# Down product of a two-level Strassen-like token pair: blocks taken in another order, closing sums split by row tile

## The chip, the cores and the metric

The kernel runs on one core of one Trainium2 chip. The metric is the device time of one execution in microseconds (us), from the kernel's runs on the chip; the median of three runs of the kernel before is 1055.15 us (1053.54 to 1056.74). The engines are named as the profile names them: PE is the matrix engine, PEld its weight loads, DVE VectorE, ACT ScalarE, POOL GpSimd and SP the engine that issues the DMAs.

## The reference

Attention with a bias, a SwiGLU layer and a SiLU layer follow each other; everything is float32. Only the last is touched here:

```python
def _moe2_ref(x, w_in, w_out):          # x: 2304 x 512, w_in: 512 x 2048, w_out: 2048 x 512
    h = x @ w_in
    g = h * (1.0 / (1.0 + np.exp(-h)))
    return (g @ w_out).astype(np.float32)

def reference(**kw):
    attn_out = _attn_ref(**attn_kwargs)  # 4 x 8 x 576 x 64
    x = attn_out.transpose(0, 2, 1, 3).reshape(B * S, H * D)
    x = _moe_ref(x=x, **moe_kwargs)      # (silu(x @ w_gate) * (x @ w_val)) @ w_out
    return _moe2_ref(x=x, **moe2_kwargs)
```

## The kernel before, in words

Attention and the SwiGLU layer take the first 655 us or so; the change touches only the last layer behind them, `up2` (L607) and `down2` (L651). Every float32 operand is held as two parts, a rounded one (the "cut", by ACT) and the remainder (one subtraction by POOL), and a product is three matmuls: rounded by rounded, rounded by remainder, remainder by rounded. A product of 2 x 2 blocks is computed with seven block products instead of eight, in sums and differences of blocks.

The tokens are done in three thirds (`TG`), each third as two halves of 384 tokens. The hidden columns go in eight steps per third, 24 steps in all. Two steps `a` and `b` and one `down2` make what is here called a **round**; there are twelve, 0 to 11, and rounds 0 to 3, 4 to 7 and 8 to 11 belong to one third each.

`up2` (one step): seven block products of 6 matmuls each, the positions xi 0 to 6, into four PSUM banks; the outputs of some are read while the bank goes on accumulating (xi 0 and 1 are copied by ACT as `s0` and `s1` at L629, and xi 2 then adds into the bank of xi 0). From the banks DVE forms `w` and `u3` (L633, L636) and adds `w` to the others in place (L639, L646), POOL adds `w` to `u3` (L637, `u <- u,w` in the trace), and ACT applies SiLU (L611), which gives `u0` to `u3`. DVE then takes differences of these: `t1 = u1 - u0` (a "token difference"), `t2 = u3 - t1`, `u1 = u3 - u1`, `t4 = u2 - t2` (`h_sub`, L605). Seven operands are cut for the down product by `h_cut` (L596: ACT at L107, then POOL at L600): B11 from `u0`, B22 from `u3`, T1 from `t1`, B21 from `u2`, T2 from `t2`, T3 from the new `u1`, T4 from `t4`. `t1`, `t2`, `t4`, `u3` and `w` have one buffer each, so the next step writes them only when the step before has been read.

`down2` (one round): seven block products, listed in `DOWN` (L42) with the name of the sum, the operand, the weight, the block and the PSUM bank. Each has two row tiles m = 0, 1 of 6 matmuls (3 for step a, 3 for step b), so the fourteen places x2m = 2x + m are 84 matmuls. Two or three products share a bank: the bank goes on accumulating, and DVE adds what it holds after each product to a sum in SBUF (`tt` at L694, `acc <- po,acc`, under the line L654 of the lambda; in rounds 0, 4 and 8 ACT copies it instead, L692). The next matmul into that bank waits for this read. When a third ends (rounds 3, 7, 11), closing sums between those SBUF sums (`close`, L662, `acc <- acc,acc`) give the four output blocks, which SP stores (L660): POOL does them for m = 0 and DVE for m = 1, in the first places of the next round, or inside `down2` in round 11.

The order on each engine is the order in which the code is written: the list `fill` (L949 to L984) hangs further work behind a place, ("u", step, xi) or ("d", round, x2m). In this way the cuts for the down product are spread, and in rounds 3 and 7 the next third's inputs are cut (`x2_cut`, L555: POOL at L560, 128 x 768), four of them at x2m 5, 7, 9 and 11.

## Time and profile before

| | |
|---|---|
| median of three runs | 1055.15 us |
| the profiled execution's own time | 1056.26 us |
| its span, first to last instruction | 1054.5 us |
| PE busy | 1012.4 us, 96% of the span |
| PEld busy | 935.4 us, 89% |
| POOL busy | 638.8 us, 61% |
| DVE busy | 584.7 us, 55% |
| ACT busy | 547.3 us, 52% |
| mean granted TensorE clock | 0.984 |

PE is nearly always busy, so the time can only move where PE waits. A row of the waits tells for how long in all, how often and at most how long an engine sat idle until another one ended. In a timeline each row has a start, a duration, the engine, the line, the operation with output <- input, and in brackets the idle time in front of it with what ended it.

### The profile page before, as it was taken

Reading aid. Unit: us, or ns where it says so; the run is one execution under the profiler, and the core shown is the slowest. Engines: PE = TensorE matmul, PEld = TensorE weight load, DVE = VectorE, ACT = ScalarE, POOL = GpSimd, SP = SyncE. Lnnn points to the kernel's source line nnn. Section 1 sums busy time; section 2 is a strip of 40 time slices with the busy share of each in tenths; the row PEclk is TensorE's granted clock in tenths of the full one; section 3 lists DMA queues with packets and bytes.
Section 4 is the critical chain, followed back from the end, with each engine's and each line's share of the span. In section 5 each row is a group of like instructions: output and inputs, shape, how many; then the busy total and the mean of one; then the engine's idle time right before and its main releaser. Section 6 shows DMA issues by size and latency. Waiting matters only on the chain.

```text
span 1054.5 us, 19518 instructions
## 1 busy us (share of the span) xinstructions
PE 1012.4 (96%) x6864; PEld 935.4 (89%) x6864; DVE 584.7 (55%) x1456; ACT 547.3 (52%) x1272; POOL 638.8 (61%) x797
## 2 busy tenths in 40 slices
PE   8889999999999999999999999999998999979997
PEld 5468998899898899898999999999998999979996
DVE  5877868635746545636533232446674466744555
ACT  6768878525665445656424542552445534455331
POOL 4667756615866656747435663655688556875456
PEclk8989999999999999999999999999998999999999
DMA  8578797758779799668486867976567765677651
GB/s 227 146 247 293 263 332 254 257 188 256 276 284 270 252 321 310 254 217 291 166 306 239 309 257 290 396 285 264 192 217 281 302 247 202 226 261 279 217 202 61
DMA packets 81618, 267.17 MB, mean 253 GB/s; under 512 B 9904, under 2 KB 29360, under 8 KB 66160
## 3 DMA queue, kind: packets, MB, share of 16 engines
q1 hardware_dynamic: 81520, 265.93, 71.7%
q8 instruction: 54, 0.88, 0.3%
q14 instruction: 44, 0.36, 0.1%
HBM read 208.15 MB, written 57.75 MB: 252 GB/s over the span
## 4 chain that ended last, share of the span: by engine, by line
PE 69%; POOL 9%; issue 5%; DMA 3%; ACT 3%; DVE 2%; POOLq 0%; SPq 0%; DVEq 0%; ACTq 0%
PE pgv L485 9%; PE pgv L487 8%; PE pgv L486 8%; POOL h L600 6%; PE po L485 5%; PE po L688 5%; PE po L486 5%; PE po L487 5%; PE po L689 4%; PE po L685 4%; PE pv L319 4%; PE psc L208 3%; PE ptr L278 3%; PE pu L623 2%; PE pu L627 2%
## 5 line engine op out<-in xcount | busy, mean ns | idle before, releaser
L485 PE MATMUL pgv<-xt,wt 128*128 128x288 f32 x768 | 230.2, 300 | 0.4 <-DVE wraw L383 0.4
L487 PE MATMUL pgv<-xt,wt 128*128 128x288 f32 x768 | 226.9, 295 | 0.0
L486 PE MATMUL pgv<-xt,wt 128*128 128x288 f32 x768 | 226.8, 295 | 0.0
L600 POOL TENSOR_TENSOR h<-u,h 128x384 fp32r<-128x384 f32 x96 | 107.4, 1123 | 110.0 <-ACT h L107 105.9
L485 PEld LDWEIGHTS pgv<-xt,wt 128*128 128x128 f32 x768 | 144.7, 188 | 11.3 <-DVE m L225 5.9
L107 ACT ACTIVATE h<-u 128x288 fp32r<-128x288 f32 (+1 forms) x192 | 92.6, 482 | 103.0 <-DVE u L497 96.5
L486 PEld LDWEIGHTS pgv<-xt,wt 128*128 128x128 f32 x768 | 144.8, 189 | 0.0
L487 PEld LDWEIGHTS pgv<-xt,wt 128*128 128x128 f32 x768 | 144.6, 188 | 0.2 <-issue 0.2
L499 POOL TENSOR_TENSOR h<-u,h 128x288 fp32r<-128x288 f32 x96 | 79.4, 830 | 88.2 <-ACT h L107 86.0
L688 PE MATMUL po<-h,wt 128*128 128x384 f32 x336 | 115.7, 344 | 15.6 <-POOL h L600 15.6
L685 PE MATMUL po<-h,wt 128*128 128x384 f32 x336 | 115.1, 343 | 3.7 <-DVE acc L654 2.2
L623 PE MATMUL pu<-x,wt 128*128 128x384 f32 x330 | 113.6, 344 | 3.8 <-ACT s L629 3.0
L485 PE MATMUL po<-h,wt 128*128 128x288 f32 x384 | 114.8, 299 | 0.0
L689 PE MATMUL po<-h,wt 128*128 128x384 f32 x336 | 114.2, 340 | 0.0
L486 PE MATMUL po<-h,wt 128*128 128x288 f32 x384 | 113.1, 295 | 0.0
L487 PE MATMUL po<-h,wt 128*128 128x288 f32 x384 | 113.0, 294 | 0.0
L627 PE MATMUL pu<-x,wt 128*128 128x384 f32 x330 | 111.7, 339 | 0.0
L626 PE MATMUL pu<-x,wt 128*128 128x384 f32 x330 | 111.7, 338 | 0.0
L238 ACT ACTIVATE e<-e,m 64x64 f32<-64x64 f32 (+4 forms) x160 | 88.3, 553 | 33.7 <-DVE m L225 29.0
L111 POOL TENSOR_SCALAR e<-e,rl 128x128 f32<-128x128 f32 (+3 forms) x128 | 69.2, 553 | 40.2 <-ACT e L238 27.8
L600 POOL TENSOR_TENSOR h<-t,h 128x384 fp32r<-128x384 f32 x72 | 81.4, 1131 | 14.4 <-ACT h L107 14.0
L654 DVE TENSOR_TENSOR acc<-po,acc 128x384 f32<-128x384 f32 x126 | 67.5, 554 | 31.4 <-PE po L689 31.3
(109 smaller groups left out, 2250.5 us busy)
## 6 DMA issues: line engine op xcount, KB each, us to landing
...
```

The costliest lines, as they stand in the source:

```text
L107: act_last[:] = [nc.scalar.activation(out=out, in_=in_, func=AF.Copy, scale=scale).ins]
L238: nc.scalar.activation(out=e[:r, hd, :wd], in_=e[:r, hd, :wd], func=AF.Exp, bias=m[hd][:r], scale=-1.0, accum_out=l[:r, hd : hd + 1],)
L485: nc.tensor.matmul(out=ps[:, :n], lhsT=a, rhs=xh, start=(k == 0), stop=False)
L486: nc.tensor.matmul(out=ps[:, :n], lhsT=a, rhs=xl, start=False, stop=False)
L487: nc.tensor.matmul(out=ps[:, :n], lhsT=c, rhs=xh, start=False, stop=(k == last))
L600: nc.gpsimd.tensor_tensor(out=h[:, 1], in0=u, in1=h[:, 0].bitcast(F32), op=ALU.subtract)
L623: nc.tensor.matmul(out=o, lhsT=a, rhs=x[:, 0, kk], start=fresh and kk == 0, stop=False, skip_group_check=True)
L626: nc.tensor.matmul(out=o, lhsT=a, rhs=x[:, 1, kk], stop=False, **more)
L627: nc.tensor.matmul(out=o, lhsT=c, rhs=x[:, 0, kk], stop=kk == 1, **more)
L685: nc.tensor.matmul(out=ps, lhsT=a, rhs=h[:, 0], start=fresh and e == 0, stop=False, skip_group_check=True)
L688: nc.tensor.matmul(out=ps, lhsT=a, rhs=h[:, 1], stop=False, **more)
L689: nc.tensor.matmul(out=ps, lhsT=c, rhs=h[:, 0], stop=e == 1, **more)
```

## The change

The second and third of the seven down products are now B22 (sum "3") and T1 (sum "35", the same bank gone on), where they were T1 (sum "5") and B22 (sum "53"). With that, POOL's addition of `w` to `u3` goes to DVE, the SiLU of `u3` and the cut of B22 come ahead of the SiLU of `u1` on ACT, the subtraction for `t1` comes behind the SiLU of `u2`, and the cuts of T1, B21, T2, T3 and T4 move one place on. Since the third sum now holds B22 + T1, the closing sums have one subtraction more for each row tile. The closing sums for m = 1 start inside `down2` of rounds 3, 7 and 11, at x2m 5, 6 and 7 on DVE; those for m = 0 stay on POOL, earlier in the next round, or behind x2m 6 in round 11.

```diff
 DOWN = [
-    ("1", "B11", "C", 0, "a"), ("5", "T1", "E", 0, "b"), ("53", "B22", "E", 3, "b"), ("12", "B21", "C", 1, "a"),
+    ("1", "B11", "C", 0, "a"), ("3", "B22", "E", 3, "b"), ("35", "T1", "E", 0, "b"), ("12", "B21", "C", 1, "a"),
...
             if xi == 4:
                 add(v, part(i, "u3"), o, u("s1"))
-                add(nc.gpsimd, u("u3"), u("u3"), u("w"))
+                add(v, u("u3"), u("u3"), u("w"))
             if xi == 5:
+                silu(u("u3"), u("u3"))
+                h_cut(i, "B22", "u3")
                 add(v, o, o, u("w"))
                 silu(part(i, "u1"), o)
-                silu(u("u3"), u("u3"))
-                h_cut(i, "B22", "u3")
             if xi == 6:
-                h_sub(i, "t1", "u1", "u0")
-                h_cut(i, "T1", "t1")
                 add(v, o, o, u("w"))
                 silu(part(i, "u2"), o)
+                h_sub(i, "t1", "u1", "u0")
...
             return {
-                0: lambda: tt(eng, F("53", m), F("53", m), F("1", m)),
...
+                0: lambda: f("3", "1", "3", ALU.subtract),
+                1: lambda: f("3", "3", "35"),
+                2: lambda: f("35", "35", "1"),
+                3: lambda: f("674", "674", "1"),
+                4: lambda: store("674", m, 1, 0),
+                5: lambda: (f("35", "35", "6"), store("35", m, 0, 1)),
+                6: lambda: (f("3", "3", "67"), store("3", m, 1, 1)),
             }[k]
...
-                if last and t == TG - 1:
-                    for f in {"53": [(g, 0), (g, 1), (g, 2)], "6": [(v, 3)], "67": [(v, 4)], "674": [(v, 5)]}.get(k, []):
-                        close(m, *f)()
-                for f in fill.get(("d", q, 2 * x + m), []):
+                x2m = 2 * x + m
+                for f in fill.get(("d", q, x2m), []):
                     f()
+                if last:
+                    for j in {5: [0], 6: [1], 7: [2, 3]}.get(x2m, []):
+                        close(1, v, j)()
...
-            put(("d", q, 2), lambda i=a: h_cut(i, "T3", "u1"))
...
+            for i, at in ((a, ("u", b)), (b, ("d", q))):
+                put((*at, 0), lambda i=i: h_cut(i, "T1", "t1"), lambda i=i: h_sub(i, "t2", "u3", "t1"))
+                put((*at, 1), lambda i=i: h_cut(i, "B21", "u2"), lambda i=i: h_sub(i, "u1", "u3", "u1"))
+                put((*at, 2), lambda i=i: h_cut(i, "T2", "t2"))
             put(("u", b, 2), lambda i=a: h_sub(i, "t4", "u2", "t2"))
...
+            put(("d", q, 3), lambda i=a: h_cut(i, "T3", "u1"))
+            put(("d", q, 4), lambda i=b: h_cut(i, "T3", "u1"))
+            put(("d", q, 5), lambda i=a: h_cut(i, "T4", "t4"), lambda i=b: h_sub(i, "t4", "u2", "t2"))
+            put(("d", q, 6), lambda i=b: h_cut(i, "T4", "t4"))
```

**What moves on DVE in every round.** The rows are DVE's from `w` of step b to its third read of a PSUM bank in `down2` (here of round 11, the others have the same), `acc2 <- po2,acc2` being those reads. Before:

```order
L612 TENSOR_TENSOR w_12708<-pu_12701,s0_12671 128x384
L612 TENSOR_TENSOR u3_12720<-pu_12713,s1_12685 128x384
L612 TENSOR_TENSOR pu_12678<-pu_12678,w_12708 128x384
L605 TENSOR_TENSOR t1_12742<-u1_12730,u0_12697 128x384
L612 TENSOR_TENSOR pu_12713<-pu_12713,w_12708 128x384
L654 TENSOR_TENSOR acc2_11835<-po2_12750,acc2_11835 128x384
L605 TENSOR_TENSOR t2_12758<-u3_12720,t1_12742 128x384
L654 TENSOR_TENSOR acc2_11853<-po2_12763,acc2_11853 128x384
L605 TENSOR_TENSOR u1_12730<-u3_12720,u1_12730 128x384
L654 TENSOR_TENSOR acc2_11866<-po2_12775,acc2_11866 128x384
```

With the change:

```order
L612 TENSOR_TENSOR u3_12724<-pu_12717,s1_12686 128x384
L612 TENSOR_TENSOR u3_12724<-u3_12724,w_12712 128x384
L612 TENSOR_TENSOR pu_12679<-pu_12679,w_12712 128x384
L612 TENSOR_TENSOR pu_12717<-pu_12717,w_12712 128x384
L605 TENSOR_TENSOR t1_12749<-u1_12738,u0_12698 128x384
L653 TENSOR_TENSOR acc2_11836<-po2_12751,acc2_11836 128x384
L605 TENSOR_TENSOR t2_12762<-u3_12724,t1_12749 128x384
L653 TENSOR_TENSOR acc2_11854<-po2_12764,acc2_11854 128x384
L605 TENSOR_TENSOR u1_12738<-u3_12724,u1_12738 128x384
L653 TENSOR_TENSOR acc2_11867<-po2_12776,acc2_11867 128x384
```

The addition of `w` to `u3` is new on DVE, and `t1` stands behind both additions into PSUM. The last row, the read of the second product's bank (m = 0), still stands behind `t1`, `t2` and the new `u1`; the third product adds into that same bank.

**What moves on DVE where a third ends.** The rows are DVE's in `down2` of round 3, with the change, from `t4` of step b (L605) to the reads of the fifth product ("6"); L663 are closing sums for m = 1. Before, `t4` and the reads followed each other with nothing between, and the closing sums came behind all reads.

```order
L605 TENSOR_TENSOR t4_11564<-u2_11489,t2_11504 128x384
L663 TENSOR_TENSOR acc2_10598<-acc2_10573,acc2_10598 128x384
L653 TENSOR_TENSOR acc2_10633<-po2_11493,acc2_10633 128x384
L663 TENSOR_TENSOR acc2_10598<-acc2_10598,acc2_10620 128x384
L653 TENSOR_TENSOR acc2_10644<-po2_11510,acc2_10644 128x384
L663 TENSOR_TENSOR acc2_10620<-acc2_10620,acc2_10573 128x384
L663 TENSOR_TENSOR acc2_10694<-acc2_10694,acc2_10573 128x384
L653 TENSOR_TENSOR acc2_10653<-po2_11595,acc2_10653 128x384
```

Four closing sums now stand ahead of the read of the fifth product's bank, into which the sixth product adds.

**What POOL does beside them.** POOL's rows in the same place with the change; `h2 <- t4` are the remainders of T4 for steps a and b, L560 the inputs of the next third, L663 the first closing sum for m = 0. Before, both T4 remainders stood ahead of the first L560 row.

```order
L600 TENSOR_TENSOR h2_11561<-t4_11445,h2_11561 128x384
L560 TENSOR_TENSOR x2_11566<-stage_11086,x2_11566 128x768
L600 TENSOR_TENSOR h2_11578<-t4_11564,h2_11578 128x384
L560 TENSOR_TENSOR x2_11590<-x2r_10742,x2_11590 128x768
L560 TENSOR_TENSOR x2_11611<-x2r_10744,x2_11611 128x768
L560 TENSOR_TENSOR x2_11628<-x2r_10744,x2_11628 128x768
L663 TENSOR_TENSOR acc2_10586<-acc2_10555,acc2_10586 128x384
```

One of the four long L560 rows has come ahead of T4 of step b; the other three still follow it.

## Rows read from the trace of the kernel before

**Rows 1.** The page's busy times: engine, us, share, instructions.

```profile
PE 1012.4 (96%) x6864; PEld 935.4 (89%) x6864; DVE 584.7 (55%) x1456; ACT 547.3 (52%) x1272; POOL 638.8 (61%) x797
```

**Rows 2.** PE's waits in the last layer: us in total, times, longest us.

```profile
PE po L688 <- POOL h L600: 15.6, 14, 2.0
PE pu L623 <- ACT s L629: 3.1, 10, 0.5
```

**Rows 3.** PE's timeline in round 10, an ordinary round.

```profile
993.90 0.45 PE L623 MATMUL pu<-x,wt 128*128 128x384 f32 x1 [0.21 <-ACT s L629]
...
999.32 0.34 PE L685 MATMUL po<-h,wt 128*128 128x384 f32 x1
...
1003.11 0.44 PE L688 MATMUL po<-h,wt 128*128 128x384 f32 x1 [0.84 <-POOL h L600]
...
1015.08 0.34 PE L623 MATMUL pu<-x,wt 128*128 128x384 f32 x1
```

**Rows 4.** ACT's timeline there: SiLU of u1, SiLU of u3, cut of B22.

```profile
999.04 0.49 ACT L611 ACTIVATE u<-pu 128x384 f32<-128x384 f32 x1 [2.73 <-DVE pu L612]
999.61 0.53 ACT L611 ACTIVATE u<-u 128x384 f32<-128x384 f32 x1
1000.16 0.53 ACT L107 ACTIVATE h<-u 128x384 fp32r<-128x384 f32 x1
```

**Rows 5.** DVE's timeline there: u3, then operations with PSUM.

```profile
997.55 0.56 DVE L612 TENSOR_TENSOR u<-pu,s 128x384 f32<-128x384 f32 x1 [0.57 <-PE pu L627]
...
1000.11 0.56 DVE L612 TENSOR_TENSOR pu<-pu,w 128x384 f32<-128x384 f32 x1
1000.58 0.55 DVE L654 TENSOR_TENSOR acc<-po,acc 128x384 f32<-128x384 f32 x1
```

**Rows 6.** POOL's timeline there: B11, the addition to u3, B22, T1.

```profile
997.60 1.01 POOL L600 TENSOR_TENSOR h<-u,h 128x384 fp32r<-128x384 f32 x1
998.56 1.01 POOL L612 TENSOR_TENSOR u<-u,w 128x384 f32<-128x384 f32 x1
1000.77 1.01 POOL L600 TENSOR_TENSOR h<-u,h 128x384 fp32r<-128x384 f32 x1 [1.20 <-ACT h L107]
1001.74 1.32 POOL L600 TENSOR_TENSOR h<-t,h 128x384 fp32r<-128x384 f32 x1
```

**Rows 7.** DVE's and POOL's timelines in round 2, at the same time.

```profile
740.46 1.35 DVE L605 TENSOR_TENSOR t<-u,t 128x384 f32<-128x384 f32 x1
...
740.38 1.01 POOL L600 TENSOR_TENSOR h<-u,h 128x384 fp32r<-128x384 f32 x1 [1.19 <-ACT h L107]
```

**Rows 8.** Round 3: PE's first down matmul; POOL; DVE.

```profile
770.30 0.34 PE L685 MATMUL po<-h,wt 128*128 128x384 f32 x1
...
778.01 1.03 POOL L600 TENSOR_TENSOR h<-t,h 128x384 fp32r<-128x384 f32 x1
...
781.31 1.87 POOL L560 TENSOR_TENSOR x<-stage,x 128x768 fp32r<-128x768 f32 x1
783.12 5.76 POOL L560 TENSOR_TENSOR x<-x2r,x 128x768 fp32r<-128x768 f32 x3
...
779.07 0.56 DVE L605 TENSOR_TENSOR t<-u,t 128x384 f32<-128x384 f32 x1 [1.85 <-POOL h L600]
...
786.60 3.99 DVE L654 TENSOR_TENSOR acc<-acc,acc 128x384 f32<-128x384 f32 x3
```

**Rows 9.** PE's waits in rounds 4 and 11, by its timeline.

```profile
804.42 0.44 PE L688 MATMUL po<-h,wt 128*128 128x384 f32 x1 [1.98 <-POOL h L600]
...
808.82 0.69 PE L688 MATMUL po<-h,wt 128*128 128x384 f32 x1 [1.01 <-POOL h L600]
...
1043.34 0.44 PE L685 MATMUL po<-h,wt 128*128 128x384 f32 x1 [2.25 <-DVE acc L654]
```

**Rows 10.** Stretches: us; PE, PEld, DVE, ACT, POOL busy (count); granted clock; DMA; GB/s.

```profile
807.00:813.00 6.00, 4.99 (x18) 4.48 (x17) 0.00 (x0) 3.63 (x9) 4.92 (x6) 0.56 0.99 406
...
1045.00:1048.00 3.00, 3.00 (x11) 3.00 (x12) 2.77 (x5) 0.00 (x0) 2.89 (x3) 0.54 0.45 164
```

More of the change, by code (lines that the diff above doesn't have):

```diff
@@ L662, in close, with f @@
         def close(m, eng, k):
+            def f(out, a, b, op=ALU.add):
+                eng.tensor_tensor(out=F(out, m), in0=F(a, m), in1=F(b, m), op=op)
             return {
-                0: lambda: tt(eng, F("53", m), F("53", m), F("1", m)),
-                1: lambda: tt(eng, F("5", m), F("5", m), F("1", m)),
-                2: lambda: tt(eng, F("674", m), F("674", m), F("1", m)),
-                3: lambda: (tt(eng, F("53", m), F("53", m), F("6", m)), store("53", m, 0, 1)),
-                4: lambda: (tt(eng, F("5", m), F("5", m), F("67", m)), store("5", m, 1, 1)),
-                5: lambda: store("674", m, 1, 0),
+                0: lambda: f("3", "1", "3", ALU.subtract),
[5 more added lines that the diff above has]
+                6: lambda: (f("3", "3", "67"), store("3", m, 1, 1)),
             }[k]
@@ L696, in down2 @@
                     store(k, m, 0, 0)
-                if last and t == TG - 1:
-                    for f in {"53": [(g, 0), (g, 1), (g, 2)], "6": [(v, 3)], "67": [(v, 4)], "674": [(v, 5)]}.get(k, []):
-                        close(m, *f)()
-                for f in fill.get(("d", q, 2 * x + m), []):
-                    f()
+                x2m = 2 * x + m
+                for f in fill.get(("d", q, x2m), []):
+                    f()
+                if last:
+                    for j in {5: [0], 6: [1], 7: [2, 3]}.get(x2m, []):
+                        close(1, v, j)()
+                    if t == TG - 1:
+                        for todo in {
+                            6: [(0, g, 0), (0, g, 1), (0, g, 2), (0, g, 3)], 9: [(0, g, 5)], 11: [(0, g, 6), (1, v, 5)],
+                            12: [(0, g, 4), (1, v, 6)], 13: [(1, v, 4)],
+                        }.get(x2m, []):
+                            close(*todo)()
         if last and t < TG - 1:
             n = 2 * q + 2
-            at = {
-                (0, 0): (0, 2), (0, 1): (0, 3), (0, 2): (0, 5), (0, 5): (0, 5), (0, 3): (0, 6), (0, 4): (1, 1),
-                (1, 0): (0, 0), (1, 1): (0, 1), (1, 2): (0, 2), (1, 5): (0, 2), (1, 3): (0, 4), (1, 4): (1, 0),
-            }
-            for (m, k), (e, xi) in at.items():
-                fill.setdefault(("u", n + e, xi), []).append(close(m, (g, v)[m], k))
+            for (e, xi), todo in {
+                (0, 0): [(1, v, 4), (0, g, 0)], (0, 1): [(1, v, 5), (0, g, 1)], (0, 2): [(1, v, 6), (0, g, 2)],
+                (0, 4): [(0, g, 3), (0, g, 4)], (0, 6): [(0, g, 5)], (1, 1): [(0, g, 6)],
+            }.items():
+                for x in todo:
+                    fill.setdefault(("u", n + e, xi), []).append(close(*x))
     steps = [(t, p) for t in range(TG) for p in range(NPR)]
@@ L956, in body @@
             a, b = 2 * q, 2 * q + 1
-            put(("u", b, 0), lambda i=a: h_sub(i, "t2", "u3", "t1"), lambda i=a: h_cut(i, "B21", "u2"))
-            put(("u", b, 1), lambda i=a: h_sub(i, "u1", "u3", "u1"), lambda i=a: h_cut(i, "T2", "t2"))
+            for i, at in ((a, ("u", b)), (b, ("d", q))):
+                put((*at, 0), lambda i=i: h_cut(i, "T1", "t1"), lambda i=i: h_sub(i, "t2", "u3", "t1"))
+                put((*at, 1), lambda i=i: h_cut(i, "B21", "u2"), lambda i=i: h_sub(i, "u1", "u3", "u1"))
+                put((*at, 2), lambda i=i: h_cut(i, "T2", "t2"))
             put(("u", b, 2), lambda i=a: h_sub(i, "t4", "u2", "t2"))
-            put(("d", q, 0), lambda i=b: h_sub(i, "t2", "u3", "t1"), lambda i=b: h_cut(i, "B21", "u2"))
-            put(("d", q, 1), lambda i=b: h_sub(i, "u1", "u3", "u1"), lambda i=b: h_cut(i, "T2", "t2"))
-            put(("d", q, 2), lambda i=a: h_cut(i, "T3", "u1"))
-            put(("d", q, 3), lambda i=b: h_cut(i, "T3", "u1"))
-            put(("d", q, 4), lambda i=a: h_cut(i, "T4", "t4"), lambda i=b: h_sub(i, "t4", "u2", "t2"))
-            put(("d", q, 5), lambda i=b: h_cut(i, "T4", "t4"))
+            put(("d", q, 3), lambda i=a: h_cut(i, "T3", "u1"))
+            put(("d", q, 4), lambda i=b: h_cut(i, "T3", "u1"))
+            put(("d", q, 5), lambda i=a: h_cut(i, "T4", "t4"), lambda i=b: h_sub(i, "t4", "u2", "t2"))
+            put(("d", q, 6), lambda i=b: h_cut(i, "T4", "t4"))
             if q > 0:
```

## The prediction

> **What bounds the kernel now.** I read the page first: PE is busy for 96% of the span and no other engine for more than 61% [rows 1], so only PE's idle times can be won or lost. Its list of waits, cut to the last layer, names two that come in every round [rows 2]: the remainder of an operand from POOL (14 times, 15.6 us) and the copy of s0 by ACT (10 times, 3.1 us). The timeline of an ordinary round shows where: 0.21 us idle in step b and 0.84 us in down, at the second product, T1 of step b [rows 3]. A wait costs more than its idle time: rows of matmuls are 0.34 us long, but the 84 of down take 15.76 us with the wait [rows 3], so 14.66 us without it, 0.1745 us each; the start is thus 0.17 us later than the idle time says, and the first matmul's row is 0.10 us longer. So 0.26 us goes on top, and the two waits cost 0.47 and 1.10 us. Dearest are the rounds where a third ends: round 4 waits 1.98 and 1.01 us, round 11 2.25 us [rows 9], and behind both the granted clock stands near its lower level for some microseconds, 0.56 and 0.54 of full speed [rows 10].
>
> **One rule of this trace decides the sum.** A DVE operation with both inputs in SBUF does not run beside a POOL operation. Asked for at 740.46, it ended at 741.81, 0.42 us behind the POOL operation that had started only 0.08 us earlier (740.38 + 1.01 = 741.39) [rows 7]. Three closing sums of DVE took 3.99 us beside POOL's long rows, which end at 788.88 [rows 8]; one and the same operation costs 0.56 us where POOL is idle (t4 at 779.07) [rows 8]. POOL's next operation is then 0.3 us longer (1.32 for 1.01) [rows 6]. Operations that read PSUM are not held: 0.56 us, 0.47 us apart [rows 5].
>
> **The ordinary rounds (1, 5, 9, 10): even.** I lay the new order on round 10's clock.
> - s0 no longer stands behind T1's cut on ACT, so step b's wait goes: -0.47, and all of down starts at 998.86.
> - u3 of step b is there at 997.55 + 0.56 - 0.47 = 997.64. The addition of w, now on DVE, is asked for at about 997.7. POOL then cuts B11 (997.60 to 998.61 [rows 6]; its queue has lost the addition of step a but gets T1 about as much later). The addition ends at 998.61 + 0.41 = 999.02. Before, POOL's ended at 999.57 [rows 6], 999.10 with the 0.47 off. Moving it wins 0.1 us.
> - On ACT, SiLU of u3 (from 999.1), its cut 0.55 later [rows 4], then SiLU of u1 0.5 later: it ends at 1000.6, where it ended at 999.53 [rows 4], 999.06 with the 0.47 off. t1 is asked for at 1000.65, 1.5 us later than before on this scale.
> - By then POOL cuts B22 (ACT's cut ends at 1000.2, POOL runs from 1000.25 to 1001.26), so t1 ends at 1001.67, and T1's remainder runs from 1002.3 to 1003.6. PE wants T1 of step b at 998.86 + 28 x 0.1745 = 1003.75 now, and B22 at 1001.65: neither is late. The wait of 1.10 us goes.
> - **What is late next:** the third product adds into the bank of the second, which DVE must have read. That read stands behind t1, a read, t2, a read and the new u1. From t1: three times 0.47 us, u1 asked for at 1003.0, held by T1's remainder until 1003.6 + 0.41, the read done at 1004.5. PE wants the bank at 998.86 + 24 x 0.1745 = 1003.05. It waits 1.5 us, 1.6 with the slower restart.
>
> Sum: -0.47 - 1.10 + 1.6 = 0. Bounds: -1.57 (no wait) and +0.5 (one more hold of 0.5). It hangs on 0.1 us: had POOL's B11 not yet started at 997.7, the addition would end 0.75 us or more sooner (see the rivals).
>
> In round 0 ACT reads the banks, so DVE's queue holds nothing: -1.0 (-1.57, with 0.5 left for ACT's own longer queue). In rounds 2 and 6 DVE also subtracts inputs of the next third; each further operation can be held once more: +1.0 each (0 to +2).
>
> **Rounds 3 and 7: 8.9 us slower each.** Times from down's first matmul. Before, POOL's cut of T4 of step a ended at 778.01 + 1.03 - 770.30 = 8.74 [rows 8]; T1's later cut makes it about 9.7. Then, in the new order:
> - POOL starts a long row at once (mean 5.76 / 3 = 1.92 us [rows 8]), to 11.6. t4 of step b, which had to wait for T4 of step a, comes just behind its start: 12.0.
> - The first closing sum finds POOL idle (12.5), a read (13.0); the second waits for T4 of step b (POOL 12.6 to 13.6): 14.0, a read (14.5).
> - The third waits for the next long row (13.6 to 15.8): 16.2. The fourth for the one behind it (to 18.0): 18.4. Then the read of the fifth product's bank, done at 18.9.
> - PE wants to add the sixth product into that bank at 60 x 0.1745 + 1.6 = 12.1. It waits 6.8 us, and with the restart 6.9. Before, nothing stood between the reads, and PE had no wait there.
> - The clock: behind waits of 2 us PE was once busy for 4.99 us with 18 matmuls, that take 3.14 at the full clock, 1.9 us lost, and once for 3.00 us with 11, 1.1 us lost [rows 10]. Behind a wait three times as long I take 2.0.
>
> Bounds: 1.7 (closing sums of 0.56 us each, the read then at 13.7) and 6.9 + 2 x 1.9 = 10.7.
>
> **Rounds 4 and 8: 5 us faster each.** Round 4 lost 1.98 + 1.01 + 2 x 0.26 [rows 9], 1.9 to the clock and up to 0.5 + 0.26 at s0 [rows 2], about 6.2 and what the clock took before that stretch, say 6.5; round 8 I take as equal. Since the closing sums of m = 1 are done and POOL's first three find it idle before the round begins, some 1.5 us are left: u3, the bank, and a sum that ACT may not overwrite before its store has landed. Bounds -3.5 and -6.5.
>
> **Round 11: 1.5 us slower.** It lost 2.25 + 0.26 [rows 9] and 1.1 for the clock, 3.6. Now, by the same steps, but with closing sums of POOL (1.0 + 0.3) in place of the long rows: t4 10.3, closing sums 10.8, 12.4, 13.7 and 15.0, the read 15.5, against 12.1. That is 3.4 + 0.1, and 1.6 for the clock. The stores behind the last matmul stay. The steps with one answer: the extra subtraction for each row tile is in these rows; loads, SP's queue and the number of matmuls stay.
>
> **The sum:** 0 - 1.0 + 2 x 1.0 + 2 x 8.9 - 2 x 5 + 1.5 = +10.3. The profiled execution took 1056.26 us, 1.1 above the median of the runs: 1066.6 for it, 1065.4 for the median. I forecast 1065.
>
> **A rule that speaks otherwise.** POOL's addition took 1.01 us [rows 6], DVE's operation of that kind 0.56 where POOL was idle and 1.35 beside it [rows 7, 8]. The Trainium skill (GPSIMD Engine Reference, Engine selection) sends an elementwise operation with two inputs to VectorE, since GpSimd is about twice as slow; by it the moved addition and each closing sum cost half of POOL's time, an estimate of 0.5 us. This is the first rival.
>
> **The rivals.**
> - **DVE is not held (0.05).** Then u3 is ready at 998.3, t1 at 1000.4, the bank is read at 1002.8, before PE wants it: -1.57 in rounds 1, 5, 9, 10, 11 and 0. Rounds 3 and 7 wait 1.7 for closing sums of 0.56 us, which the 1.57 pays; round 11 wins 2 more, rounds 2 and 6 win 0.5 each. With -10 for rounds 4 and 8 that is -23: 1032. Rows 7 and 8 speak against it.
> - **The closing sums miss the long rows (0.14), faster.** If POOL's long rows come so late or early that the four sums find it idle, the bank read is at 13.7 and rounds 3 and 7 cost 1.7 for 8.9: +10.3 - 14.4 = -4.1, so 1051. It decides at a wait below some 3.5 us there. Against it: the rows' inputs are cut by ACT long before, and POOL's queue has no gap.
> - **A boundary falls the other way (0.20).** If the addition slips in ahead of B11, the bank comes 0.9 us sooner in rounds 1, 5, 9, 10 and 11: 1061. For it: 0.1 us decides.
> - **Ordinary rounds lose no time at all, but the closing sums do (0.07).** -1.57 in six rounds: +10.3 - 8.4, so 1057.
>
> **The numbers.** The forecast has 0.54: its own range is 1060 to 1073, from 8.9 less 2 in two rounds to the upper bounds of rounds 3, 7 and 4. The range leaves out the first two rivals (0.19) and reaches from 1053 to 1073. Faster by over 0.3% (3.2 us, about what a measurement of this kernel can tell): the first two rivals and a little of the last, 0.20. Within 0.3%: most of the last and a mix, 0.08. Slower: 0.72.
>
> **What would show it.** Right: no wait of PE's for POOL's T1 in ordinary rounds, in its place one of some 1.3 us for DVE's read of a bank at the third product; in rounds 3 and 7 one wait of 6 to 7 us for DVE's read at the sixth product, with four closing sums of 0.5 to 2.3 us in front of it on DVE; in rounds 4 and 8 no wait above 1.5 us. Wrong: DVE's closing sums at 0.56 us beside POOL's long rows, or PE's longest wait below 3.5 us.

## The result, and the profile after

The changed kernel took **1066.83 us**, median of three runs (1066.73 to 1068.54), against 1055.15 (1053.54 to 1056.74): a ratio of **1.0116**, 95% interval 1.0087 to 1.0145. The forecast was 1065, slower. The profiled execution took 1068.54 us, 12.3 above that of before, with a span of 1066.7 us. The busy times of its page:

```profile
PE 1010.6 (95%) x6864; PEld 937.1 (88%) x6864; DVE 611.8 (57%) x1484; ACT 547.2 (51%) x1272; POOL 610.2 (57%) x775
```

DVE's busy time grew by 27 us and POOL's fell by 29 [rows 1]; PE has the same 6864 matmuls, so the difference is looked for in its idle time and its clock. PE's four largest waits in the last layer (us in total, times, longest), to be read beside [rows 2]:

```profile
PE po L688 <- DVE acc L653: 29.8, 14, 6.8
PE pu L623 <- DVE u L612: 4.2, 6, 1.2
PE po L688 <- ACT acc L107: 0.9, 2, 0.7
PE po L688 <- DMA wt<-wu_d: 0.6, 2, 0.4
```

The wait for POOL's T1 is gone and so is the one for s0. In their place stands the read of a PSUM bank by DVE. (L688, L691, L692 are the three matmuls of down, L685, L688, L689 before; L653 the bank reads, L663 the closing sums.)

Where the 12.3 us lie is read from PE's timeline: the length of each round, from the first up matmul of its step a to that of the next round (round 11: to one matmul's step, 0.18 us, behind the start of the last matmul). 168 matmuls at the 0.1752 us by which they follow each other where nothing waits make 29.43 us, here called the floor; what a round takes beyond that is what it loses.

```
us per round      0     1,5,9,10   2, 6    3, 7    4, 8    11     all twelve
                        (mean)    (mean)  (mean)  (mean)
before          31.16    31.12    32.09   31.19   36.26   35.35   390.05
after           30.77    31.03    34.23   40.13   31.60   36.29   403.09
difference      -0.39    -0.09    +2.14   +8.94   -4.66   +0.94   +13.04
forecast        -1.0      0       +1.0    +8.9    -5      +1.5    +10.3
```

What comes ahead of round 0, which the change does not touch, was 0.9 us shorter, so 12.1 of the 12.3 us are left; what comes behind the last matmul is as long as before (4.0 us for 3.9). **Round 3** of the changed kernel, by its timelines: PE's first down matmul and its wait, then DVE, then POOL.

```profile
770.66 0.34 PE L688 MATMUL po<-h,wt 128*128 128x384 f32 x1
...
789.53 0.66 PE L688 MATMUL po<-h,wt 128*128 128x384 f32 x1 [6.79 <-DVE acc L653]
...
780.46 2.19 DVE L605 TENSOR_TENSOR t<-u,t 128x384 f32<-128x384 f32 x1 [1.30 <-POOL h L600]
782.57 0.55 DVE L663 TENSOR_TENSOR acc<-acc,acc 128x384 f32<-128x384 f32 x1
783.04 0.54 DVE L653 TENSOR_TENSOR acc<-po,acc 128x384 f32<-128x384 f32 x1
783.50 1.25 DVE L663 TENSOR_TENSOR acc<-acc,acc 128x384 f32<-128x384 f32 x1
784.67 0.55 DVE L653 TENSOR_TENSOR acc<-po,acc 128x384 f32<-128x384 f32 x1
785.14 3.77 DVE L663 TENSOR_TENSOR acc<-acc,acc 128x384 f32<-128x384 f32 x2
788.84 1.01 DVE L653 TENSOR_TENSOR acc<-po,acc 128x384 f32<-128x384 f32 x2
...
779.41 1.01 POOL L600 TENSOR_TENSOR h<-t,h 128x384 fp32r<-128x384 f32 x1
780.39 1.84 POOL L560 TENSOR_TENSOR x<-stage,x 128x768 fp32r<-128x768 f32 x1
...
783.34 1.00 POOL L600 TENSOR_TENSOR h<-t,h 128x384 fp32r<-128x384 f32 x1 [1.11 <-ACT h L107]
784.30 6.29 POOL L560 TENSOR_TENSOR x<-x2r,x 128x768 fp32r<-128x768 f32 x3
```

The same operation took 0.55 us where POOL was idle (782.57), 1.25 beside a POOL row of 1.00 (784.75 is 0.41 behind that row's end), and 3.77 for two beside the long rows. Behind them stands the read at 788.84, for which PE waits 6.79 us. Round 7 has the same wait, 6.80. The clock behind it, and behind the wait of round 11 (columns as in [rows 10]):

```profile
790.00:797.00 7.00, 7.00 (x31) 7.00 (x30) 2.59 (x5) 0.00 (x0) 3.56 (x4) 0.71 0.06 8
1056.50:1063.00 6.50, 5.97 (x24) 5.68 (x24) 3.37 (x8) 0.00 (x0) 3.39 (x4) 0.74 0.24 86
```

PE stood idle for 6.79 us before the first stretch; in it the granted clock is 0.50 of full speed up to 794, which is the lower of its two levels (1.2 GHz), and full from 795 on. From 789.53 to the next round at 795.88 are 6.35 us for 24 matmuls, that take 4.2 at 0.1752: 2.1 us more are lost there. **Round 10**, an ordinary one: PE's first down matmul and its one long wait, DVE from the addition of w to u3, POOL's B11, B22, T1 and the row behind it.

```profile
1010.09 0.34 PE L688 MATMUL po<-h,wt 128*128 128x384 f32 x1
...
1015.62 0.44 PE L688 MATMUL po<-h,wt 128*128 128x384 f32 x1 [1.21 <-DVE acc L653]
...
1008.90 1.24 DVE L612 TENSOR_TENSOR u<-u,w 128x384 f32<-128x384 f32 x1
...
1011.79 1.08 DVE L605 TENSOR_TENSOR t<-u,u 128x384 f32<-128x384 f32 x1 [0.72 <-ACT u L611]
...
1014.20 0.90 DVE L605 TENSOR_TENSOR u<-u,u 128x384 f32<-128x384 f32 x1
1015.02 1.01 DVE L653 TENSOR_TENSOR acc<-po,acc 128x384 f32<-128x384 f32 x2
...
1008.72 1.00 POOL L600 TENSOR_TENSOR h<-u,h 128x384 fp32r<-128x384 f32 x1
...
1011.45 1.01 POOL L600 TENSOR_TENSOR h<-u,h 128x384 fp32r<-128x384 f32 x1 [1.73 <-PE po L692]
...
1013.51 1.17 POOL L600 TENSOR_TENSOR h<-t,h 128x384 fp32r<-128x384 f32 x1 [1.05 <-ACT h L107]
1014.63 1.32 POOL L600 TENSOR_TENSOR h<-u,h 128x384 fp32r<-128x384 f32 x1
```

Three DVE rows with both inputs in SBUF end 0.42, 0.41 and 0.42 us behind the POOL row beside them (1009.72, 1012.46, 1014.68). In the whole last layer of this kernel 80 such rows of 384 columns start while a row of POOL's runs, and all end 0.41 or 0.42 us behind it. The two reads of a PSUM bank at 1015.02 are not held: 1.01 us for both, beside POOL's row of 1.32 (1014.63). The Trainium skill (SBUF — State Buffer, Who interferes with whom) states that a DVE instruction with two SBUF inputs contends with a GpSimd instruction that reads SBUF. By the Trainium skill (SBUF — State Buffer, SBUF: two separate sides) whichever of the two starts first has the shared pair of ports for the whole instruction. These rows agree. What one collision costs, the rest of POOL's row plus 0.41 us, is read from the rows.

Last, PE's timeline in rounds 2, 4 and 11:

```profile
737.07 0.44 PE L623 MATMUL pu<-x,wt 128*128 128x384 f32 x1 [1.22 <-DVE u L612]
...
751.36 0.41 PE L688 MATMUL po<-h,wt 128*128 128x384 f32 x1 [1.45 <-DVE acc L653]
...
810.33 0.44 PE L623 MATMUL pu<-x,wt 128*128 128x384 f32 x1 [0.51 <-DVE u L612]
...
816.92 0.44 PE L688 MATMUL po<-h,wt 128*128 128x384 f32 x1 [0.67 <-ACT acc L107]
...
1056.73 0.51 PE L688 MATMUL po<-h,wt 128*128 128x384 f32 x1 [3.54 <-DVE acc L653]
```

Round 2 has two waits that it did not have before; round 4 has none above 0.7 us where it had 1.98 and 1.01 [rows 9].

### The profile page after: what moved, and what is told of

Its sections match the earlier page's. It is cut to its first block, busy times and chain, and to the rows that moved or that the text cites. A ratio compares the mean times of both kernels' runs of the same rounds, so it can differ in the third digit from the quotient of the medians.

```text
span 1066.7 us, 19533 instructions
## 1 busy us (share of the span) xinstructions
PE 1010.6 (95%) x6864; PEld 937.1 (88%) x6864; DVE 611.8 (57%) x1484; ACT 547.2 (51%) x1272; POOL 610.2 (57%) x775
## 4 chain that ended last, share of the span: by engine, by line
PE 73%; DVE 6%; POOL 4%; issue 4%; ACT 2%; DMA 2%; DVEq 0%; POOLq 0%; ACTq 0%
PE pgv L485 9%; PE pgv L487 9%; PE pgv L486 9%; PE po L485 5%; PE po L486 5%; PE po L487 5%; PE pv L319 4%; PE pu L623 4%; PE pu L627 4%; PE pu L626 4%; PE po L688 3%; PE psc L208 3%; PE po L691 3%; PE po L692 3%; PE ptr L278 3%
## 5 line engine op out<-in xcount | busy, mean ns | idle before, releaser
L600 POOL TENSOR_TENSOR h<-u,h 128x384 fp32r<-128x384 f32 x96 | 104.6, 1094 | 130.1 <-ACT h L107 112.1
L688 PE MATMUL po<-h,wt 128*128 128x384 f32 x336 | 117.3, 349 | 31.4 <-DVE acc L653 29.8
L691 PE MATMUL po<-h,wt 128*128 128x384 f32 x336 | 115.1, 343 | 0.3 <-POOL h L600 0.3
L692 PE MATMUL po<-h,wt 128*128 128x384 f32 x336 | 114.7, 341 | 0.0
L600 POOL TENSOR_TENSOR h<-t,h 128x384 fp32r<-128x384 f32 x72 | 78.5, 1091 | 38.3 <-ACT h L107 23.1
L688 PEld LDWEIGHTS po<-h,wt 128*128 128x128 f32 x336 | 64.8, 193 | 38.2 <-issue 18.0
```

The lines of the kernel that those rows point to most:

```text
L600: nc.gpsimd.tensor_tensor(out=h[:, 1], in0=u, in1=h[:, 0].bitcast(F32), op=ALU.subtract)
L688: nc.tensor.matmul(out=ps, lhsT=a, rhs=h[:, 0], start=fresh and e == 0, stop=False, skip_group_check=True)
L691: nc.tensor.matmul(out=ps, lhsT=a, rhs=h[:, 1], stop=False, **more)
L692: nc.tensor.matmul(out=ps, lhsT=c, rhs=h[:, 0], stop=e == 1, **more)
```

## The experiments

Eleven kernels, each a variant of the changed one. Ratios are to the kernel before in the same session, with 95% intervals. The medians of before in the sessions were 1054 to 1057 us, and single runs of one kernel spread by up to 1.2%, so the readings rest on the round lengths of the profiles, one execution of each kernel. These differ by 0.3 us or less between most rounds of one kind (at most by 2.0, rounds 4 and 8 of e11):

```
us per round        0     1,5,9,10  2, 6   3, 7   4, 8    11    all    time    ratio
e1 close next     30.79    31.02   34.22  32.81  35.67  34.77  395.0  1062.3  1.0055 (1.0034-1.0076)
e2 quarter sums   30.77    31.02   34.24  36.92  31.76  36.16  396.8  1065.0  1.0078 (1.0052-1.0105)
e3 u3 on POOL     31.71    31.95   34.95  40.94  33.20  38.22  415.9  1080.8  1.0233 (1.0188-1.0277)
e4 reads first    30.80    31.20   36.19  40.36  31.88  36.40  408.9  1072.3  1.0163 (1.0118-1.0209)
e5 and t4 late    30.11    29.76   32.68  35.81  31.41  33.73  382.6  1049.7  0.9951 (0.9925-0.9976)
e6 SiLU u1 first  30.15    30.55   32.80  40.61  31.59  35.51  397.8  1062.1  1.0081 (1.0053-1.0109)
e7 close late     30.77    31.02   34.24  32.84  33.34  31.29  387.0  1056.4  1.0020 (1.0003-1.0036)
e8 late all       30.36    29.77   31.69  31.45  32.94  33.21  374.8  1042.7  0.9881 (0.9857-0.9904)
e9 short rows     30.81    31.04   34.24  36.13  31.49  36.34  395.0  1060.2  1.0056 (1.0035-1.0077)
e10 spread sums   30.40    29.75   31.68  31.76  31.65  30.46  370.0  1040.5  0.9856 (0.9811-0.9900)
e11 t4a later     29.94    29.48   31.38  31.44  32.61  30.15  368.9  1040.1  0.9853 (0.9810-0.9896)
```

The table ends with the last matmul. From its end to the end of the span are 3.9 us before, 4.0 after and 4.0 to 5.3 in the variants, but 8.3 in e7, e10 and e11: there closing sums of DVE and POOL, late and side by side, reach past the last matmul. So much of what round 11 wins in those three comes back behind it.

**e1: DVE's closing sums of rounds 3 and 7 back in the next round.**

```diff
-                if last:
+                if last and t == TG - 1:
...
-                (0, 0): [(1, v, 4), (0, g, 0)], (0, 1): [(1, v, 5), (0, g, 1)], (0, 2): [(1, v, 6), (0, g, 2)],
-                (0, 4): [(0, g, 3), (0, g, 4)], (0, 6): [(0, g, 5)], (1, 1): [(0, g, 6)],
+                (0, 0): [(1, v, 0), (0, g, 0)], (0, 1): [(1, v, 1), (0, g, 1)],
+                (0, 2): [(1, v, 2), (1, v, 3), (1, v, 4), (0, g, 2)],
+                (0, 4): [(1, v, 5), (0, g, 3), (0, g, 4)], (0, 6): [(0, g, 5)], (1, 0): [(1, v, 6)], (1, 1): [(0, g, 6)],
```

> Edit: in rounds 3 and 7 the closing sums for m = 1 go back to the first places of the next round on DVE; all else as changed. Theory (the four closing sums, each held beside POOL's long rows, stand ahead of DVE's read of the fifth product's bank): PE's two waits of 6.8 us at the sixth product fall below 1.5 us and their slow clock goes, about 9 us for each third; rounds 4 and 8 get some 2 us each back, since POOL's rows then reach into them. Time 1051 to 1055 us. Rival (the wait comes from the cuts of T4 and the long rows themselves, not from the closing sums): the two waits stay above 4 us, time above 1060 us.

The waits of 6.8 us fell to 1.48 and 1.47, and rounds 3 and 7 are 7.3 us shorter: these sums held the read for 5.3 of the 6.8 us. But rounds 4 and 8 are 4.1 us longer, more than expected, and the time missed its range. The wait that is left in round 3, and four of the six sums in one run on DVE ahead of step a's w, still beside POOL:

```profile
783.49 0.41 PE L688 MATMUL po<-h,wt 128*128 128x384 f32 x1 [1.48 <-DVE acc L653]
...
788.44 4.91 DVE L663 TENSOR_TENSOR acc<-acc,acc 128x384 f32<-128x384 f32 x4
793.27 0.54 DVE L612 TENSOR_TENSOR w<-pu,s 128x384 f32<-128x384 f32 x1
```

PE's own waits come later: 1.89 us for u at step b's position xi 6, and 0.80 (1.90 in round 8) for ACT's copy at the third product.

**e2 and e9: are the sums held, or only many?** In e2 the sums work on a quarter of the columns, in e9 POOL's long rows do; the rest of those sums and remainders is left out.

```diff
 e2, close()
-                eng.tensor_tensor(out=F(out, m), in0=F(a, m), in1=F(b, m), op=op)
+                n = TN // 4 if m == 1 and k < 4 and t < TG - 1 else TN
+                eng.tensor_tensor(out=F(out, m)[:, :n], in0=F(a, m)[:, :n], in1=F(b, m)[:, :n], op=op)
 e9, x2_cut()
-        eng.tensor_tensor(out=x[:, 1], in0=src, in1=x[:, 0].bitcast(F32), op=ALU.subtract)
+        n = TN // 4 if i > 2 and t > 0 else TN
+        eng.tensor_tensor(out=x[:, 1, :, :n], in0=src[:, :, :n], in1=x[:, 0, :, :n].bitcast(F32), op=ALU.subtract)
+        if n < TN:
+            copy("a", x[:, 1, :, n:], src[:, :, n:])
```

> Edit: the four closing sums for m = 1 inside down of rounds 3 and 7 take 96 of the 384 columns; the rest of these sums is left out. Theory (a closing sum ends when POOL's operation beside it ends, and only the last 0.41 us are its own): each held sum ends some 0.3 us earlier, the two waits of 6.8 us fall to 5.3 to 6.2 us, time 1063 to 1066 us. Rival (the sums cost by their own length): their 5.6 us fall to a quarter, the waits to below 3.5 us, time below 1060 us.

> After as it is, but POOL's four long rows in down of rounds 3 and 7 (128 x 768, some 2 us each) compute 192 of their 768 columns; ACT fills the rest of that operand with a copy of the input, so that those remainders are left out of the computation. The closing sums of DVE are untouched. Theory (the sums are held by the long rows beside them): each sum takes 0.6 to 1.1 us where it took up to 1.9, and the wait at the sixth product of rounds 3 and 7 falls from 6.8 us to 1.5 to 3.5; those rounds lose 4 to 6.5; time 1055 to 1060. Rival (the wait comes from the number of DVE operations in front of the read, or from t4, not from what POOL does): the wait stays above 5 us and the time above 1063.

In e2 a quarter sum took 0.24 us alone, 0.61 where it met POOL's cut of T4, and 1.86 where it met a long row; DVE, then POOL:

```profile
785.89 0.24 DVE L664 TENSOR_TENSOR acc<-acc,acc 128x96 f32<-128x96 f32 x1
...
787.70 1.86 DVE L664 TENSOR_TENSOR acc<-acc,acc 128x96 f32<-128x96 f32 x1
...
787.62 1.82 POOL L560 TENSOR_TENSOR x<-x2r,x 128x768 fp32r<-128x768 f32 x1
```

So the length of a held sum is POOL's, not its own; it ends 0.12 us behind POOL's row where a full one ends 0.41 behind. The wait was 4.1 us, between the two expectations (the time, 1065.0, is in the theory's range): the shorter sums come earlier, and meet one long row less. In e9 the full sums took 1.41 us for two beside the shortened rows, in place of 3.77, and the wait fell to 3.24 (3.20 in round 7), in the theory's range; the rounds lost 6.7 us and the time was 1060.2, both a little above it. Of the 3.6 us by which the wait fell, 1.2 are t4, which took 0.94 us beside the first shortened row where it took 2.19.

```profile
780.09 1.41 DVE L666 TENSOR_TENSOR acc<-acc,acc 128x384 f32<-128x384 f32 x2
...
782.12 0.41 PE L691 MATMUL po<-h,wt 128*128 128x384 f32 x1 [3.24 <-ACT x L107]
```

(The bank read that the matmul also needs is the first half of a DVE row from 781.43 to 782.44; the label names ACT's fill, which only this kernel has.)

**e3: the addition of w to u3 back on POOL.**

```diff
-                add(v, u("u3"), u("u3"), u("w"))
+                add(nc.gpsimd, u("u3"), u("u3"), u("w"))
```

> Edit: the addition of w to u3 goes back to POOL; all else as changed. Theory (on DVE it is held until POOL has cut B11, so that u3 is ready within 0.1 us of when POOL's own addition was): rounds 1, 5, 9, 10 keep a wait of 1.0 to 1.5 us at the third product, time 1064 to 1069 us. Rival (the moved addition is what makes DVE late): that wait falls below 0.7 us, time below 1063 us.

Ordinary rounds became 0.92 us longer, which neither side expected; the wait at the third product, 1.44, is in the theory's range, the time 12 us above it. On POOL the addition stands behind a run of cuts and ends 15.97 us after the round's start (1006.31); on DVE, in the changed kernel, 14.92 (1008.90 + 1.24, start 995.22):

```profile
1020.30 1.00 POOL L600 TENSOR_TENSOR h<-u,h 128x384 fp32r<-128x384 f32 x1
1021.28 1.00 POOL L612 TENSOR_TENSOR u<-u,w 128x384 f32<-128x384 f32 x1
```

The Trainium skill (Perfetto Trace Analysis, Optimizing Scalar/DVE Operations) warns that work moved between GpSimd and DVE may not help since they share a read port. Here it did, by 1.05 us, although the addition was held on DVE (1.24 for 0.55): POOL's queue was the longer one.

**e4 and e5: DVE's reads ahead of step b's t2 and new u1 (e4), and of its t4 (e5, both edits).**

```diff
-            for i, at in ((a, ("u", b)), (b, ("d", q))):
-                put((*at, 0), lambda i=i: h_cut(i, "T1", "t1"), lambda i=i: h_sub(i, "t2", "u3", "t1"))
-                put((*at, 1), lambda i=i: h_cut(i, "B21", "u2"), lambda i=i: h_sub(i, "u1", "u3", "u1"))
+            for i, at, e in ((a, ("u", b), 0), (b, ("d", q), 2)):
+                put((*at, 0), lambda i=i: h_cut(i, "T1", "t1"))
+                put((*at, e), lambda i=i: h_sub(i, "t2", "u3", "t1"))
+                put((*at, 1), lambda i=i: h_cut(i, "B21", "u2"))
+                put((*at, e + 1), lambda i=i: h_sub(i, "u1", "u3", "u1"))
...
 e5 only
-            put(("d", q, 5), lambda i=a: h_cut(i, "T4", "t4"), lambda i=b: h_sub(i, "t4", "u2", "t2"))
-            put(("d", q, 6), lambda i=b: h_cut(i, "T4", "t4"))
+            put(("d", q, 5), lambda i=a: h_cut(i, "T4", "t4"))
+            put(("d", q, 8), lambda i=b: h_sub(i, "t4", "u2", "t2"), lambda i=b: h_cut(i, "T4", "t4"))
```

> Edit: in step b, t2 and the new u1 are subtracted behind DVE's reads of the second product's bank (places 2 and 3 of down in place of 0 and 1). Theory (the read stands behind two held operations on DVE): the waits of 1.2 us at the third product go (below 0.2 us) in rounds 1, 5, 9, 10, 11; in rounds 3, 7 and 11 the wait at the sixth product grows by as much, since DVE's chain there hangs on POOL and not on PE. Time 1059 to 1063 us. Rival (PE then waits for T1's or T2's remainder instead, which POOL cuts no earlier): below 2 us gained, time above 1064.5 us.

> As in the run with the reads first (step b's t2 and new u1 one or two places later, behind DVE's reads of the banks), and besides t4 of step b and its cut go from the sixth and seventh place to the ninth, so that no read stands behind a t4 that waits for POOL's cut of T4 of step a. Theory (in an ordinary round PE waits for whichever read stands behind a held subtraction; with both of these moved no read does): no wait for DVE's read at the third nor at the sixth product, ordinary rounds lose 0.3 to 0.8 us where after loses 1.6, rounds 2 and 6 about 2 us where after loses 4.8; rounds 3 and 7 keep the closing sums and lose 9 to 11. Time 1055 to 1060. Rival (the DVE queue as a whole is late, and whatever comes behind the held subtractions waits): one wait of 1 us or more stays in the ordinary rounds, at another place, and they lose 1.5 us or more; time 1066 or above.

e4 missed on the slow side. The wait at the third product went, and one of 1.19 us came at the sixth: t4 of step b waits for POOL's cut of T4 of step a, and four reads stand behind it. In rounds 3, 7 and 11 the wait at the sixth product grew by 1.3 to 1.4 us, about as expected.

```profile
1027.66 0.56 DVE L605 TENSOR_TENSOR t<-u,t 128x384 f32<-128x384 f32 x1 [2.66 <-POOL h L600]
1028.14 1.95 DVE L653 TENSOR_TENSOR acc<-po,acc 128x384 f32<-128x384 f32 x4
...
1029.76 0.41 PE L688 MATMUL po<-h,wt 128*128 128x384 f32 x1 [1.19 <-DVE acc L653]
```

With t4 behind the reads as well (e5) ordinary rounds lose 0.33 us, where the changed kernel loses 1.60 and the one before 1.69: neither wait of the new order is needed there. The time, below the range, is less than before's, since rounds 3 and 7 gained too (no t4 ahead of the closing sums): they lose 6.4 us for 9 to 11 expected. Rounds 2 and 6 lose 3.2, more than the 2 expected.

**e6: SiLU of u1 ahead of that of u3.** On ACT the SiLU of u1 comes first, then SiLU of u3 and B22's cut; on DVE the addition of w to u3 comes behind the first addition into PSUM, and t1 is subtracted ahead of the last one.

```diff
-                add(v, u("u3"), u("u3"), u("w"))
             if xi == 5:
-                silu(u("u3"), u("u3"))
-                h_cut(i, "B22", "u3")
                 add(v, o, o, u("w"))
+                add(v, u("u3"), u("u3"), u("w"))
                 silu(part(i, "u1"), o)
+                silu(u("u3"), u("u3"))
+                h_cut(i, "B22", "u3")
             if xi == 6:
+                h_sub(i, "t1", "u1", "u0")
                 add(v, o, o, u("w"))
                 silu(part(i, "u2"), o)
-                h_sub(i, "t1", "u1", "u0")
```

> The SiLU of u1 goes ahead of the SiLU of u3 and its cut on ACT, and t1 is subtracted ahead of the last addition into PSUM on DVE; B22 is still the second product and T1 the third. Theory (the wait at the third product comes from t1, which is 1.5 us later than before because ACT makes u3 and its cut first): the wait for DVE's read at the third product falls from 1.2 us to 0.5 or less, ordinary rounds lose 0.5 to 0.9 us where after loses 1.6, rounds 2 and 6 gain as much; B22 is still there in time; time 1056 to 1062 at 1066.8 for after. Rival (t1, t2 and the new u1 are held one after the other by POOL's operations whenever they are asked for): ordinary rounds stay within 0.3 us of after's 1.6, or PE waits for B22 in place of the read, 0.5 us or more.

The wait at the third product fell from 1.21 to 0.37 us, and t1 ended 1.62 us sooner (16.03 after the round's start at 989.58, 17.65 after that at 995.22 in the changed kernel):

```profile
1005.05 0.56 DVE L605 TENSOR_TENSOR t<-u,u 128x384 f32<-128x384 f32 x1 [0.17 <-ACT u L611]
...
1009.44 0.44 PE L688 MATMUL po<-h,wt 128*128 128x384 f32 x1 [0.37 <-DVE acc L653]
```

That the new order on ACT and DVE together makes t1 late by some 1.5 us is shown. What ACT's order alone does was not run: in e6 the SiLU of u1 also no longer stands behind the held addition of w to u3, and t1 misses POOL's cut of B22 (0.56 us for 1.08). The rounds lost 1.1 us, a little more than the 0.5 to 0.9 expected; the time, 1062.1, is 0.1 above the range.

**e7: DVE's closing sums late inside down.**

```diff
-                    for j in {5: [0], 6: [1], 7: [2, 3]}.get(x2m, []):
+                    for j in ({11: [0], 12: [1], 13: [2, 3]}, {9: [0], 10: [1], 11: [2, 3]})[t == TG - 1].get(x2m, []):
```

> The closing sums of DVE (m = 1) stay inside down of rounds 3, 7 and 11 but come at the places 11, 12 and 13 (9, 10 and 11 in round 11), behind the read of the fifth product's bank. Theory (the 6.8 us are the read standing behind four held sums, not the sums' work): the waits at the sixth product of rounds 3 and 7 go below 1 us, those rounds lose 2 to 4 us where after loses 10.7; rounds 4 and 8 lose 2 to 5, since the last sums now run into them, still beside POOL's long rows; round 11 loses 3 to 5 where after loses 6.9, with a longer end. Time 1050 to 1058. Rival (the sums only move the wait: the seventh product's reads or the next round's w stand behind them and cost as much): rounds 3 and 4 together lose 11 us or more, where after loses 13.1, and the time stays above 1062.

The theory held in the main: rounds 3 and 7 lose 3.4 us and rounds 4 and 8 3.9, as expected, and the time is in its range. The wait at the sixth product fell to 1.47 us, not below 1: as in e1, t4 beside the long row is left. Round 11 loses 1.9, less than expected, but 4.3 us more pass behind its last matmul. The sums are all there and beside POOL; behind the fifth product's read they cost 5.6 us less over rounds 3 and 4 than ahead of it. In round 4 the last of them stand in front of step a's w:

```profile
790.63 4.76 DVE L663 TENSOR_TENSOR acc<-acc,acc 128x384 f32<-128x384 f32 x4
795.31 0.54 DVE L612 TENSOR_TENSOR w<-pu,s 128x384 f32<-128x384 f32 x1
```

**e8, e10, e11: the edits together.** e8 is e5 with e7, and DVE's second subtraction for the next third (128 x 768) at the end of down; e10 spreads the sums, e11 moves t4 of step a.

```diff
 e8, to e5 and e7
-            for at, k in ((-2, 3), 1), ((-2, 6), 2), ((0, 2), 3), ((0, 5), 4):
+            for at, k in ((-2, 3), 1), ((0, 2), 3), ((0, 5), 4):
+            put(("d", q - 1, 13), lambda t=t: x2_sub(t, 2))
 e10, to e8
-                    for j in ({11: [0], 12: [1], 13: [2, 3]}, ...
+                    for j in ({10: [0], 11: [1], 12: [2], 13: [3]}, ...
-                            6: [(0, g, 0), (0, g, 1), (0, g, 2), (0, g, 3)], 9: [(0, g, 5)],
+                            6: [(0, g, 0), (0, g, 1)], 9: [(0, g, 2), (0, g, 3), (0, g, 5)],
 e11, to e10
-            put(("u", b, 2), lambda i=a: h_sub(i, "t4", "u2", "t2"))
+            put(("u", b, 5), lambda i=a: h_sub(i, "t4", "u2", "t2"))
```

> The edits that removed waits put together: step b's t2 and new u1 behind DVE's reads, t4 of step b in the ninth place, DVE's closing sums late (places 11 to 13, and 9 to 11 in round 11), and besides DVE's second subtraction of inputs for the next third (128 x 768) goes from step a to the end of down in rounds 2 and 6, where it held up w and u3 of step b by 1.2 us. Theory (each of these waits is a held DVE operation in front of something that PE wants, and they are independent): ordinary rounds lose 0.3, rounds 2 and 6 1.5 to 2, rounds 3 and 7 1 to 2.5, rounds 4 and 8 3.5 to 4.5, round 11 0.5 to 1.5, 14 to 20 us together where after loses 50; time 1035 to 1044, faster than both kernels. Rival (the late reads and the late closing sums get in each other's way in rounds 3 and 7, since t4 now stands between them): those rounds lose over 5 us, time 1046 to 1050, no better than the run with t4 late alone.

> As the run with the late edits together, but DVE's closing sums of rounds 3 and 7 come at the places 10, 11, 12 and 13, one behind each read, and POOL's four closing sums of round 11 come two at the seventh place and two at the tenth, ahead of and behind the cut of T4 of step b. Theory (what is left in rounds 4 and 8 is w behind the last sums, and in round 11 T4's cut behind POOL's sums): the wait for u at the start of rounds 4 and 8 falls from 1.4 us to 0.6 or less, the wait of 1.9 us for POOL's T4 in round 11 goes; rounds 4 and 8 lose 2.3 to 2.8, round 11 1.0 to 2.2; together 3 to 4.5 us off. Rival (the earlier sum delays the read of the eleventh or twelfth place, and so the seventh product): rounds 3 and 7 lose 1 us or more in addition, and the sum over the rounds stays within 1.5 us.

> As the run with spread sums, and besides t4 of step a is subtracted behind the first addition into PSUM of step b's sixth position and no longer ahead of step b's w. Theory (t4 of step a is one more held operation in front of w and u3): the waits for u in rounds 2, 4, 6 and 8 (0.4 and 0.7 us) go, these rounds lose 0.4 to 0.9 less each, ordinary rounds stay within 0.1: 2 to 3 us off. Rival (t4 then holds up step b's u2 and t1, whose reads of the banks follow): ordinary rounds lose 0.5 us or more each, and the time is longer than without this edit.

e8 took 1042.7 us, faster than both kernels; the gains nearly added up (21.6 us lost over all rounds, for 14 to 20 expected), and the wait of 1.22 us in round 2 went with the moved subtraction. Two rows of its PE timeline say what was left, in rounds 4 and 11:

```profile
789.29 0.44 PE L623 MATMUL pu<-x,wt 128*128 128x384 f32 x1 [1.41 <-DVE u L612]
...
1030.49 0.44 PE L691 MATMUL po<-h,wt 128*128 128x384 f32 x1 [1.92 <-POOL h L600]
```

The second was not expected (round 11 lost 3.8, for 0.5 to 1.5): t4 in the ninth place puts its cut behind POOL's four closing sums. e10 removed both, 4.8 us over the rounds for the 3 to 4.5 expected; but 2.9 of them came back behind the last matmul (8.3 us for 5.3), and the times of e8 and e10 can't be told apart (their intervals overlap). e11 brings ordinary rounds to 0.05 us above the floor, but only 1.1 us in all for the 2 to 3 expected: the waits of 0.4 in rounds 2 and 6 stayed, in rounds 4 and 8 PE now waits 1.1 us for a remainder of POOL's, and in round 4 1.7 for a copy of ACT's that round 8 lacks; why was not tried. Two of its waits:

```profile
PE po L691 <- POOL h L600: 3.1, 4, 1.1
PE po L688 <- ACT acc L107: 1.7, 1, 1.7
```

The times of e10 and e11 can't be told apart either; both are 1.5% below before. Whether the order of before, with its own subtractions and sums put behind the reads in the same way, would gain as much was not run.

## Why the prediction was right, by its steps

- **The rule** (a DVE operation with two SBUF inputs ends 0.41 us behind the POOL operation that it meets): right in every row read, for 384 columns; e2 and e9 show it from both sides. That reads of PSUM are not held was right too, but the rows given for it do not show it: the two rows of [rows 5] that are 0.47 us apart start while POOL is idle. The rows at 1015.02 and 1014.63 above show it. And of the three closing sums in [rows 8], which end at 790.59, the last stood beside a closing sum of POOL's and not beside a long row; nothing hangs on that.
- **Rounds 3 and 7** (+8.9, measured +8.94), step by step on the clock from down's first matmul at 770.66: t4 done at 12.0 (782.65), the first sum at 12.5 (783.12), the second at 14.1 (784.75) for 14.0, the fourth at 18.3 (788.91) for 18.4, the read at 18.7 for 18.9, the wait 6.79 for 6.8. Clock and restart took 2.1, as put. e1, e7 and e9 take away the sums, their place, or what holds them, and the wait falls to 1.48, 1.47 and 3.24. The first two say that t4 beside the long row, which the prediction has as a step of the same chain, is 1.5 of the 6.8.
- **Ordinary rounds** (even, measured -0.09): both old waits went and a new one of 1.21 came, for 1.5. The addition ended 0.05 us behind down's start (forecast 0.16), t1 2.78 (2.81), the read some 5.5 (5.6). That t1 is late by the new order on ACT and DVE is shown by e6, that the reads wait for what stands in front of them by e4 and e5.
- **"Moving it wins 0.1 us" was wrong**: e3 gives 1.05. That step set POOL's addition 0.47 sooner with PE's clock, but in e3 the addition stands behind four of POOL's cuts in a row (1016.83 to 1021.30), so it hangs on POOL's own queue and not on PE. It was a comparison beside the sum, whose own times were those of the new order; so it did no harm.
- **Rounds 2 and 6** (+1.0, bounds 0 to +2; measured +2.14): mis-sized. "Each further operation can be held once more" priced one hold; there were two waits. The 1.22 at step b's position xi 6 is the 128 x 768 subtraction in front of w (e8 moves it and the wait goes). The 1.45 at the sixth product is t4, which takes 2.17 us beside a long POOL row ahead of T4 of step b, like the one that the order showed for round 3, with four reads behind it (e5 moves t4, and one wait of 0.66 is left in round 2, two of 0.40 or less in round 6):

```profile
747.64 2.17 DVE L605 TENSOR_TENSOR t<-u,t 128x384 f32<-128x384 f32 x1 [1.30 <-POOL h L600]
749.74 1.94 DVE L653 TENSOR_TENSOR acc<-po,acc 128x384 f32<-128x384 f32 x4
```

  The same chain was worked out for round 3 and not carried to round 2.
- **Rounds 4 and 8** (-5, measured -4.66): right, with the waits that were left as named, u3 (0.5 us) and the sum that ACT may not overwrite (0.7 in round 4, 0.2 in round 8). In round 4 that sum's store, issued at 810.24, landed at 816.28, and ACT's copy started at 816.38.
- **Round 11** (+1.5, measured +0.94): the wait of 3.54 (for 3.4) and 1.6 us for the clock were right; the loss before was 4.2 us (35.35 against 31.12), not 3.6.
- **Round 0** (-1.0, measured -0.39): mis-sized. Two waits for weights, 0.6 us together (`DMA wt<-wu_d` above), stand there, which were not thought of. They need not be the cause: in e4 and e9 the round is as long (30.80 and 30.81) with no wait for weights and one of 0.5 us for ACT's copy at the sixth product. Which of the two it is stays open.
- **The rivals**: DVE not held and the sums missing the long rows are out by the rows above; with POOL's rows shortened (e9) rounds 3 and 7 are 4.0 us shorter each, in the direction of the latter. (The first rival's terms add to -22.4, not -23.) The boundary fell as forecast, by a small margin: POOL's B11 started 0.18 us ahead of the addition (1008.72 and 1008.90). That ordinary rounds lose nothing was not so by 1.6 us, but e5 shows that it was two moves of order away, with 0.33 left.
- **The sum** (+10.3 for the rounds, measured +13.0): the misses have both signs, and rounds 2 and 6 are the largest part (+2.3). That the profiled execution came within 2 us of its forecast (1068.5 for 1066.6) has a little luck in it: 0.9 us less ahead of round 0 hid a part of the miss.
